# K and V gradient stores on ScalarE's DMA queue, K and V loads alone on SyncE's

## Chip, core and metric

The kernel runs on one core of one Trainium2 chip. The metric is the device time of one execution in microseconds (us). Before the change it is 723.07 us, the median of 3 runs (722.93 to 723.51).

## What is computed

The reference is one decode step of a block that adds attention over a KV cache and a gated MLP to its input, together with the gradients of everything for a given `grad_out`. One token (a row of 640) meets 32 heads with a cache of 8192 x 128 each, in bf16.

```python
q = (xn @ wq).reshape(1, 1, 32, 128)                     # xn = layernorm(x)
scores = einsum("bhqd,bhkd->bhqk", q, k) * 128 ** -0.5   # k, v: [1, 32, 8192, 128]
p = softmax(scores)
out = x + einsum("bhqk,bhkd->bhqd", p, v).reshape(1, 1, 4096) @ wo
out = out + (silu(xn @ w1) * (xn @ w3)) @ w2
outputs = out, *vjp(grad_out)     # d x, d k_cache, d v_cache, d wq, d wo, d w1, d w3, d w2
```

The gradients of K and V are as large as the caches: each head reads 2 MB of K and 2 MB of V and writes 2 MB of each gradient. With the weights and their gradients that is 151.34 MB read and 152.91 MB written.

## The kernel before

**Slots.** Ten SBUF slots of [128, 8192] bf16 (`kv0` to `kv9`, 2 MB each, L133) hold K and V tiles. A tile is loaded into a slot, used, overwritten in place by its own gradient and stored; then the slot takes another load. Four of the slots hold the MLP's weights first, until `mlp()` has run, between heads 1 and 2.

**One head** is written out by hand in `head(h)` (L834); the schedule is manual, so every engine runs its instructions in the order in which the code issues them. K is transposed in eight chunks of four 128x128 blocks by TensorE (`T`, L400 to L407) into one of three PSUM buffers `pT`, which ScalarE copies to SBUF (`KT`, L406); `Mp` (L425) multiplies the copies with the query and accumulates the scores; ScalarE takes them out (`ev`, L432). V goes the same way with the output gradient. VectorE does the softmax (row maximum `mx`, L468). The first four chunks of the next head's K are transposed already at the end of a head. The sums over the cache (`wsum`, L519) are matmuls on the untransposed tiles.

**Gradients.** `outer` (L552) overwrites a tile with an outer product on VectorE, in two halves of 2.28 us. At the start of head h VectorE does both halves of head h-1's V and the first half of its K (`outers_a`, L822); the second half of K follows after head h's softmax (`outers_b`, L828). The cast of the next query rows `qd` (`rows_act`, L462) on ScalarE comes behind that.

**Stores and loads.** `store` (L563) is called at the end of `outers_a` for V and of `outers_b` for K. It puts the gradient's store on SyncE's DMA queue (`fifo`, L106), gives the slot back to the list `free_slots` and calls `load_next` (L139), which puts the next pending K or V load on the same queue (`fifo_wide`, L111; head 0 by L106) into the slot that has been free longest. After the first loads `lag[0]` is 3: a load is only issued while at least three slots are free, so its slot's store lies two stores back. SyncE issues its DMAs in order; a load first waits until the store of its slot has landed, and whatever stands behind it waits too. From head 23 on each of 15 stores is followed by a marker: a load of 1 to 15 rows of 8 bytes of `A_x` into a small tile `marks`, which nothing reads.

**Completion.** DMAs issued by SyncE and ScalarE take turns on eight completion semaphores; a DMA that reuses one waits for the earlier DMA on it.

**Other queues.** POOL (GpSimd) issues the MLP's gradients, the weights of the later groups of four heads, and the weight gradients. The gradient of wq leaves for most groups as scatters (L372), six of `wq_g` and `rel` tiles in turn and one more for `rel`, each behind the landing of the one before; the work for one group is spread over the heads of the next (`side_k`, `side_m`, `side_v`, L770 to L803). VectorE writes `rel` at L601, and needs the scatter that read it last to have landed. ScalarE's queue carries only the two input rows at the start.

Of the kernel before, what the change touches and what calls it, by code (L numbers as in the profile page):

```python
# [9 lines left out]
BF16 = mybir.dt.bfloat16  # L10
# [11 lines left out]
def kernel(  # L22
# [22 lines left out]
    nc = tc.nc  # L45
# [14 lines left out]
    consts = ctx.enter_context(tc.tile_pool(name="consts", bufs=1))  # L60
# [16 lines left out]
    dkc = out_2.rearrange("b h (p j) d -> (b h) p (j d)", p=P)  # L77
    dvc = out_3.rearrange("b h (p j) d -> (b h) p (j d)", p=P)
# [26 lines left out]
    def fifo(out_, in_):  # L105
        nc.sync.dma_start(out_, in_)  # L106
# [21 lines left out]
        load_wq(g, eng)  # L128
        load_wo(g, eng)

    x_rows = A_x.rearrange("a b (k w) -> (a b k) w", w=40)
    marks = consts.tile([16, 15, 4], BF16, name="marks")
    free_slots = [kvpool.tile([P, KVN], BF16, name=f"kv{i}", tag=f"kv{i}") for i in range(NSLOT)]  # L133
    kv_tiles = {}
    pending = [("K", h) if k == 0 else ("V", h) for h in range(H) for k in range(2)]

    lag = [1]

    def load_next():  # L139
        if not pending or len(free_slots) < lag[0]:  # L140
            return
        kind, h = pending.pop(0)
        t = free_slots.pop(0)
        (fifo if h == 0 else fifo_wide)(t[:], (kc if kind == "K" else vc)[h])
        kv_tiles[(kind, h)] = t
# [28 lines left out]
    fifo(w3b, w3_v[:, NA, :])  # L174
    for _ in range(2):
        load_next()

    lag[0] = 3

    ident_f = consts.tile([P, P], F32, name="ident_f")  # L180
    make_identity(nc, ident_f[:])
# [49 lines left out]
    def pst():  # L231
        return ps_t.tile([P, 512], F32, name="pT", tag="pT")
# [40 lines left out]
    def prep_do(g, hh):  # L273
        G_ = grp[g]
        junk = small.tile([P, D], BF16, name="side", bufs=1)
        nc.vector.scalar_tensor_tensor(junk[:], G_["wo"][:, hh, :], 1.0, g_bc[:], ALU.mult, ALU.mult,  # L276
                                       accum_out=G_["do"][:, hh:hh + 1])
        if hh == GH - 1:
            nc.vector.tensor_copy(G_["cb"][:, 1, :], G_["do"][:])
# [117 lines left out]
    def new_head(h):  # L397
        hd[h] = dict(kt={}, qz=qz_tiles[h % 2])

    def T(h, kind, c):  # L400
        W3 = kv_tiles[(kind, h)][:].bitcast(F32).rearrange("p (i w) -> p i w", w=P)
        pT = pst()
        for k in range(4):
            nc.tensor.transpose(pT[:, k * P:(k + 1) * P], W3[:, 4 * c + k, :], ident_f[:])  # L404
        KT = kt_tile()
        nc.scalar.copy(KT[:].rearrange("p k w -> p (k w)"), pT[:])  # L406
        hd[h]["kt"][(kind, c)] = KT  # L407
# [21 lines left out]
    def ev(h, kind):  # L429
        S_ = hd[h]  # L430
        XS = kt_tile()
        nc.scalar.copy(XS[0:QH].rearrange("p k w -> p (k w)"), S_.pop(kind)[0:QH, :])  # L432
        S_["xr" + kind] = XS
# [26 lines left out]
    def rows_act(h):  # L460
        qd = small.tile([P, 2, DH], BF16, name="qd")
        nc.scalar.copy(qd[:].rearrange("p a d -> p (a d)"), hd[h].pop("ps_r"))  # L462
        hd[h]["qd"] = qd
# [63 lines left out]
    def o_sum(h):  # L527
        wsum(h, "V", 0)
# [12 lines left out]
    def col(h):  # L541
        g = h // GH
        m = hd[h]["m"]
        XS = xg.pop("XS")
        for r in range(4):
            nc.tensor.matmul(m[:, OC:OC + NS], lhsT=XS[:, r, :], rhs=mask8[:, r, :],
                             start=False, stop=(r == 3), skip_group_check=True)
        nc.scalar.copy(grp[g]["od"][:].rearrange("p h a -> p (h a)"), m[:, OC:OC + NS])

    def outer(dst, vec, pair, lo, hi):  # L550
        n = hi - lo
        nc.vector.tensor_tensor(  # L552
            dst[:, lo * DH:hi * DH].rearrange("p (j a b) -> p j a b", a=DH // 2, b=2),
            vec.rearrange("p (a b) -> p a b", b=2).unsqueeze(1).to_broadcast([P, n, DH // 2, 2]),
            pair[:, lo:hi, :].unsqueeze(2).to_broadcast([P, n, DH // 2, 2]), ALU.mult)

    def outer_v(h, lo, hi):
        outer(kv_tiles[("V", h)], hd[h]["qd"][:, 1, :], hd[h]["P2"], lo, hi)

    def outer_k(h, lo, hi):  # L560
        outer(kv_tiles[("K", h)], hd[h]["qd"][:, 0, :], hd[h]["U2"], lo, hi)

    def store(kind, h):  # L563
        t = kv_tiles.pop((kind, h))
        if kind == "K":
            hd.pop(h)
        fifo((dkc if kind == "K" else dvc)[h], t[:])
        n = 2 * (h - 23) + (kind == "K") + 1
        if 1 <= n <= 15:
            fifo(marks[0:n, n - 1, :], x_rows[0:n, 0:4])  # L570
        free_slots.append(t)
        load_next()

    dxa = consts.tile([P, NC, NG], F32, name="dxa")

    def fin_od(g):
        G_ = grp[g]
        G_["od_bf"] = small.tile([P, GH, 2], BF16, name="od_bf")
        nc.vector.tensor_scalar(G_["od_bf"][:, :, 0:1], G_["od"][:, :, 0:1], 1.0, None, ALU.mult)
        nc.vector.tensor_scalar(G_["od_bf"][:, :, 1:2], G_["od"][:, :, 1:2], scale, None, ALU.mult)  # L580
# [23 lines left out]
    def fin_wq(g, ci):  # L604
        G_ = grp[g]
        wq_g, dqb = G_["wq"], G_["dqb"]
        nc.vector.scalar_tensor_tensor(wq_g[:, ci, :], wq_g[:, ci, :], 1.0, dqb, ALU.mult, ALU.mult,  # L607
                                       accum_out=dxa[:, ci, g:g + 1])
        nc.vector.tensor_scalar(wq_g[:, ci, :], dqb, xn_col[:, ci:ci + 1], None, ALU.mult)
        if g in SCAT:  # L610
            scatter(wq_g[:, ci, :], row_idx[:, ci:ci + 1], g)
            if ci == NC - 1:
                rel_out(g, 1)
        elif g == 0:
            nc.gpsimd.dma_start(dwq_v[:, ci, 0:GW], wq_g[:, ci, :])
        elif ci == NC - 1:
            nc.gpsimd.dma_start(dwq_v[:, :, g * GW:(g + 1) * GW], wq_g[:])
        if ci == NC - 1:
            grp.pop(g)
            if g + 3 < NG:  # L620
                load_group(g + 3, nc.gpsimd)
# [148 lines left out]
    def side_k(h):  # L770
        g, hh = divmod(h, GH)
        if hh == 1 and g > 0:
            fin_wq(g - 1, 0)
        elif hh == 2 and g > 0:
            fin_wq(g - 1, 3)
        elif hh == 3 and g + 1 < NG:
            prep_do(g + 1, 1)
# [44 lines left out]
    def outers_a(h):  # L822
        outer_v(h, 0, J // 2)
        outer_v(h, J // 2, J)
        store("V", h)
        outer_k(h, 0, J // 2)

    def outers_b(h):  # L828
        outer_k(h, J // 2, J)
        store("K", h)  # L830
# [3 lines left out]
    def head(h):  # L834
        nxt = h + 1 < H
        pre = nxt and h + 1 != MLP_AT
        has_prev = h > 0 and h != MLP_AT
        had = (4 if h else 2) if h != MLP_AT else 0
        if nxt:
            new_head(h + 1)  # L840
        if has_prev:
            outers_a(h - 1)
        side_k(h)
        for c in range(had, NCH, 2):
            T(h, "K", c)
            T(h, "K", c + 1)
            if c >= 2:
                Mp(h, "K", c - 2)
            if h > 0 and h % GH == 0 and c == 4:
                col(h - 1)  # L850
        T(h, "V", 0)
        T(h, "V", 1)
        Mp(h, "K", NCH - 2)
        ev(h, "K")
        if h == 0:
            first_do()
        T(h, "V", 2)
        T(h, "V", 3)
        selm(h, "K")
        mx(h)  # L860
        Mp(h, "V", 0)
        T(h, "V", 4)
        mx_bc(h)
        side_m(h)
        T(h, "V", 5)
        Mp(h, "V", 2)
        expo(h)
        T(h, "V", 6)
        zsum(h)
        probs(h)  # L870
        if has_prev:
            outers_b(h - 1)
        side_pe1(h)
        T(h, "V", 7)
        side_pe1b(h)
        Mp(h, "V", 4)
        side_pe2(h)
        side_v(h)
        if nxt:
            fill_qz(h + 1)  # L880
            rows_pe(h + 1, pst()[:, 0:2 * DH], True)
            rows_act(h + 1)
        if pre:
            T(h + 1, "K", 0)
            T(h + 1, "K", 1)
        Mp(h, "V", NCH - 2)
        ev(h, "V")
        o_sum(h)
        selm(h, "V")
        rdot(h)  # L890
        if pre:
            T(h + 1, "K", 2)
        dsum(h)
        if pre:
            T(h + 1, "K", 3)
            Mp(h + 1, "K", 0)
        dq_sum(h)
        if not nxt:
            col(h)
# [12 lines left out]
    for h in range(H):  # L912
        if h == 6:
            rel_setup()
        if h == MLP_AT:
            outers_a(h - 1)
            outers_b(h - 1)
            mlp()
        head(h)
        if h < 2:  # L920
            nc.gpsimd.tensor_copy(gate[:], hd[h]["rdot"][:])
            load_group(h + 1, nc.gpsimd)
    outers_a(H - 1)
    outers_b(H - 1)
    fin_od(NG - 1)
    fin_pe(NG - 1)
    fin_wo(NG - 1)
# [65 lines left out]
```

## Time and profile before

| | |
|---|---|
| median of 3 runs | 723.07 us (722.93 to 723.51) |
| profiled execution | 722.83 us; span from first to last instruction 721.0 us |
| TensorE busy | 602.1 us (84%), granted clock 0.928 of full on average |
| VectorE busy | 472.2 us (65%) |
| ScalarE busy | 364.3 us (51%) |
| POOL busy | 85.1 us (12%) |
| DMA | 303.56 MB, mean 421 GB/s |
| K and V loads, stores | 64 and 64 of 2048 KB each |
| chain that ended last | DMA 45%, TensorE 39%, VectorE 10% |

The profile comes from one execution on the chip. Its page gives busy time by engine, the span in 40 slices of 18 us with the tenths in which each engine was busy and the GB/s that the DMA engines moved, the DMA queues (q1 is the queue of SyncE, q0 that of POOL), the chain of work that ended last, and the costliest groups of instructions. The trace behind it gives the same for any window: a timeline (start, duration, engine, line, operation, output <- input), the waits (who waited for whom) and busy times by stage. In a timeline PE is TensorE, DVE is VectorE, ACT is ScalarE, and SPq is SyncE's queue. A bracket at the end of a line tells how long the engine was idle before the instruction and what ended that.

### The profile page before, as it was taken

To read this page: it belongs to the slowest core of one execution; us is meant where nothing else is said; L and a number is where in the kernel's file an instruction comes from. 1 tells how busy PE (TensorE), PEld (TensorE's weight loads), DVE (VectorE), ACT (ScalarE), POOL (GpSimd) and SP (SyncE) were. 2 spreads that over 40 slices of the span, in tenths; PEclk is the share of its full clock that TensorE was granted. 3 is DMA by queue.
4 is the path that set the end of the run, shared out by engine and by line. 5 is a ranking of instruction groups with operands and counts; after the bars stand their busy time and mean duration, and the time that the engine had idled before them with its cause. 6 is when DMAs were issued, how large, how long until landed. Compare 5 with 4: busy or idle time off the path is not lost.

```text
span 721.0 us, 13243 instructions
## 1 busy us (share of the span) xinstructions
PE 602.1 (84%) x5237; PEld 376.9 (52%) x5244; DVE 472.2 (65%) x895; ACT 364.3 (51%) x726; POOL 85.1 (12%) x86
## 2 busy tenths in 40 slices
PE   6989699987999999878986899778987889978921
PEld 4556566645565556545553555445554555545510
DVE  4369927678858886767755765556774757667581
ACT  3641166653666566545554555455653556555510
POOL 0110100000101122111120111112210101111110
PEclk9987999997999999999998999899998999999965
DMA  9999999999999999999999999999999999999996
GB/s 358 400 418 413 437 428 424 425 436 428 420 425 422 431 429 428 418 434 431 423 423 430 423 430 427 423 429 430 430 419 430 427 432 427 428 432 425 424 428 295
DMA packets 23403, 303.56 MB, mean 421 GB/s; under 512 B 4054, under 2 KB 5404, under 8 KB 10156
## 3 DMA queue, kind: packets, MB, share of 16 engines
q1 hardware_dynamic: 16840, 276.39, 90.1%
q0 software_dynamic: 6496, 26.31, 9.1%
q8 instruction: 41, 0.67, 0.4%
q14 instruction: 22, 0.18, 0.1%
q10 hardware_dynamic: 4, 0.00, 0.0%
HBM read 151.34 MB, written 152.91 MB: 422 GB/s over the span
## 4 chain that ended last, share of the span: by engine, by line
DMA 45%; PE 39%; DVE 10%; ACT 3%; issue 2%; SPq 0%; ACTq 0%; DVEq 0%
DMA kv<-in_A_k_cache_dram 27%; PE pT L404 18%; DMA out_dram<-kv 13%; PE sA L425 5%; DVE kv L552 4%; PE dA L425 4%; PE X L519 4%; DMA kv<-in_A_v_cache_dram 3%; PE m L442 2%; ACT KT L406 2%; DMA out_dram<-rel,rel_idx 1%; PE gu_ps L649 1%; PE dh_ps L660 1%; PE dx_acc L747 1%; ACT KT L432 1%
## 5 line engine op out<-in xcount | busy, mean ns | idle before, releaser
L406 ACT COPY KT<-pT 128x512 f32<-128x512 f32 x512 | 288.2, 588 | 235.4 <-PE pT L404 214.8
L404 PE MATMUL pT<-ident_f,kv 128*128 128x128 f32 x2048 | 304.3, 287 | 53.9 <-DMA kv<-in_A_k_cache_dram 39.8
L404 PEld LDWEIGHTS pT<-ident_f,kv 128*128 128x128 f32 x2048 | 233.9, 147 | 144.2 <-PE pT L404 52.9
L552 DVE TENSOR_TENSOR kv<-qd,U 128x4096 bf16<-128x4096 bf16 x64 | 146.0, 2284 | 0.0
L552 DVE TENSOR_TENSOR kv<-qd,P 128x4096 bf16<-128x4096 bf16 x64 | 143.6, 2284 | 0.0
L519 PE MATMUL X<-kv,Z 128*32 128x512 bf16 x1024 | 96.8, 413 | 1.8 <-DVE Z L536 1.8
L425 PE MATMUL dA<-KT,qz 128*32 128x512 bf16 x512 | 84.9, 411 | 0.0
L425 PE MATMUL sA<-KT,qz 128*32 128x512 bf16 x512 | 82.0, 400 | 0.0
L372 POOL DMA_INDIRECT out_dram<-wq_g,row_idx x30 | 43.1, 1437 | 283.3 <-DMA out_dram<-wq_g,row_idx 108.0
L502 DVE SCALAR_TENSOR_TENSOR U<-m,P 128x64 bf16<-128x64 f32 x32 | 7.5, 235 | 94.3 <-PE m L442 94.3
L519 PEld LDWEIGHTS <-Z 128*32 128x32 bf16 x1024 | 32.7, 101 | 36.2 <-issue 9.4
L425 PEld LDWEIGHTS <-qz 128*32 128x32 bf16 x1024 | 29.5, 95 | 41.0 <-issue 38.1
L442 PEld LDWEIGHTS m<-selc,KT 64*128 64x128 f32 x256 | 21.1, 141 | 30.1 <-ACT KT L432 19.4
L442 PE MATMUL m<-selc,KT 64*128 64x64 f32 x256 | 30.0, 239 | 8.0 <-ACT KT L432 8.0
L468 DVE TENSOR_REDUCE mrow<-m 128x1 f32<-128x64 f32 x32 | 7.1, 223 | 41.7 <-PE m L442 41.4
L372 POOL DMA_INDIRECT out_dram<-rel,rel_idx x12 | 15.1, 1260 | 142.3 <-DVE rel L601 59.0
L462 ACT CAST qd<-pT 128x256 bf16<-128x256 f32 x32 | 11.9, 373 | 38.2 <-DVE kv L552 30.4
L475 DVE TENSOR_REDUCE negM<-m 128x1 f32<-128x128 f32 x32 | 9.3, 292 | 32.2 <-PE m L472 32.2
L276 DVE SCALAR_TENSOR_TENSOR side<-wo_g,g_bc 128x640 bf16<-128x640 bf16 x32 | 26.2, 819 | 2.3 <-DMA wo_g<-in_A_wo_dram 2.0
L607 DVE SCALAR_TENSOR_TENSOR wq_g<-wq_g,side 128x512 bf16<-128x512 bf16 x40 | 27.3, 683 | 0.0
L534 DVE SCALAR_TENSOR_TENSOR U<-m,P 128x128 bf16<-128x128 f32 x32 | 11.4, 355 | 15.5 <-PE m L532 15.5
L432 ACT COPY KT<-dA 64x512 f32<-64x512 f32 x32 | 18.6, 582 | 4.5 <-PE dA L425 4.5
(179 smaller groups left out, 403.9 us busy)
## 6 DMA issues: line engine op xcount, KB each, us to landing
out_dram<-kv SPq DMA_DIRECT2D x64, 2048.0 KB
kv<-in_A_k_cache_dram SPq DMA_DIRECT2D x32, 2048.0 KB
kv<-in_A_v_cache_dram SPq DMA_DIRECT2D x32, 2048.0 KB
out_dram<-wo_g POOLq DMA_DIRECT2D x8, 640.0 KB, 15.6
wq_g<-in_A_wq_dram POOLq DMA_DIRECT2D x7, 640.0 KB, 16.2
wo_g<-in_A_wo_dram POOLq DMA_DIRECT2D x7, 640.0 KB, 22.6
kv<-in_B_w_dram SPq DMA_DIRECT2D x2, 1728.0 KB
out_dram<-kv POOLq DMA_DIRECT2D x2, 1728.0 KB, 30.8
```

The source lines that it names most:

```text
L276: nc.vector.scalar_tensor_tensor(junk[:], G_["wo"][:, hh, :], 1.0, g_bc[:], ALU.mult, ALU.mult, accum_out=G_["do"][:, hh:hh + 1])
L372: nc.gpsimd.indirect_dma_start(dwq_row, bass.IndirectOffsetOnAxis(ap=idx, axis=0), src, None, element_offset=g * GW, bounds_check=(D - 1) ...
L404: nc.tensor.transpose(pT[:, k * P:(k + 1) * P], W3[:, 4 * c + k, :], ident_f[:])
L406: nc.scalar.copy(KT[:].rearrange("p k w -> p (k w)"), pT[:])
L425: nc.tensor.matmul(S_[kind][q:q + QW, :], lhsT=S_["qz"][:, o:o + QW], rhs=KTb[c][:, par, :], start=(c0 == 0 and par == 0), stop=(c0 == NCH ...
L432: nc.scalar.copy(XS[0:QH].rearrange("p k w -> p (k w)"), S_.pop(kind)[0:QH, :])
L442: nc.tensor.matmul(S_["m"][:, b0:b0 + 4 * J].rearrange("p (x c k t) -> p k x c t", x=4, k=4, t=2)[:, k], lhsT=XS[0:QH, k, :], rhs=selc[0:Q ...
L462: nc.scalar.copy(qd[:].rearrange("p a d -> p (a d)"), hd[h].pop("ps_r"))
L519: nc.tensor.matmul(xg["X"][q:q + QW, :], lhsT=Z[:, o:o + QW], rhs=W[:, N4 * i:N4 * (i + 1)], start=(slot == 0 and i < 4), stop=(slot == NS ...
L534: nc.vector.scalar_tensor_tensor(S_["U2"][:], S_["V"][:, 0:J].unsqueeze(2).to_broadcast([P, J, 2]), S_["m"][:, OC + NS:OC + NS + 1], S_["P ...
L552: nc.vector.tensor_tensor(dst[:, lo * DH:hi * DH].rearrange("p (j a b) -> p j a b", a=DH // 2, b=2), vec.rearrange("p (a b) -> p a b", b=2 ...
L607: nc.vector.scalar_tensor_tensor(wq_g[:, ci, :], wq_g[:, ci, :], 1.0, dqb, ALU.mult, ALU.mult, accum_out=dxa[:, ci, g:g + 1])
```

## The change

`store` no longer issues anything: it notes the finished tile in a list `made`. A new function `send` empties the list. For each tile it issues the store on ScalarE's DMA queue, gives the slot back and calls `load_next`. `send` is called twice in a head: behind `side_k` (so on ScalarE behind the copies of the first four chunks of K, and ahead of the others), which takes the V store, and behind `rows_act`, which takes the K store; and it is called ahead of the MLP and at the end. `load_next` issues a load as soon as one slot is free. The slot is then the one whose store was issued just before, and SyncE waits until that store has landed. SyncE's queue carries no stores of K and V any more. The markers are gone. The order on TensorE, VectorE and POOL is unchanged.

```diff
-    x_rows = A_x.rearrange("a b (k w) -> (a b k) w", w=40)
-    marks = consts.tile([16, 15, 4], BF16, name="marks")
...
-    lag = [1]
-
     def load_next():
-        if not pending or len(free_slots) < lag[0]:
+        if not pending or not free_slots:
             return
...
-    lag[0] = 3
-
...
+    made = []
+
     def store(kind, h):
-        t = kv_tiles.pop((kind, h))
+        made.append((kind, h, kv_tiles.pop((kind, h))))
         if kind == "K":
             hd.pop(h)
-        fifo((dkc if kind == "K" else dvc)[h], t[:])
-        n = 2 * (h - 23) + (kind == "K") + 1
-        if 1 <= n <= 15:
-            fifo(marks[0:n, n - 1, :], x_rows[0:n, 0:4])
-        free_slots.append(t)
-        load_next()
+
+    def send():
+        while made:
+            kind, h, t = made.pop(0)
+            nc.scalar.dma_start((dkc if kind == "K" else dvc)[h], t[:])
+            free_slots.append(t)
+            load_next()
...
         side_k(h)
+        send()
         for c in range(had, NCH, 2):
...
             rows_act(h + 1)
+        send()
         if pre:
...
             outers_b(h - 1)
+            send()
             mlp()
...
     outers_a(H - 1)
+    send()
     outers_b(H - 1)
+    send()
```

## Prediction

> **What bounds the kernel now.** I read the page's slices first (part 2: DMA share and GB/s in 40 slices).
>
> ```profile
> DMA  9999999999999999999999999999999999999996
> GB/s 358 400 418 413 437 428 424 425 436 428 420 425 422 431 429 428 418 434 431 423 423 430 423 430 427 423 429 430 430 419 430 427 432 427 428 432 425 424 428 295
> ...
> q1 hardware_dynamic: 16840, 276.39, 90.1%
> q0 software_dynamic: 6496, 26.31, 9.1%
> ```
>
> The DMA engines are full in every slice but the last. 303.56 MB at the usual 427 GB/s is 711 us of the 721.0 us span; the start (77 GB/s in the first 3 us) and the end (298 GB/s at 712 to 716 us, 60 at 716 to 721) take the rest. So the first bound is bytes, and the change moves the same bytes, the markers apart. Second, the waits, by engine and line (us in total, times, longest):
>
> ```profile
> SPq L111 <- DMA out_dram<-kv: 452.5, 56, 14.1
> ...
> PE pT L404 <- DMA kv<-in_A_k_cache_dram: 39.8, 19, 4.7
> ```
>
> SyncE stands 452 us before loads, waiting for a slot's store, and the next store waits behind it; yet TensorE lacks only 40 us of K (and 13.8 of V). Third, how much room compute has. In the chain of waits no K or V load stands between 11.7 and 301.6 us: there compute runs freely. VectorE's timeline gives the start of each head's V gradient (L552, P): 186.88, 204.70, 222.81, 240.03, 257.25, so four free heads in 70.37 us, **17.6 us a head**. From the one at 105.82 to the last at 687.30 are 29 heads in 581.5 us, 20.05 each. The head with rel_setup took 28.3, 10.7 extra. So 581.5 - 29 x 17.6 - 10.7 = 60 us is slack, **2.08 us a head**. That is the number that decides this case.
>
> **The change, part by part.**
>
> *64 stores move from SyncE to ScalarE.* ScalarE now waits for what the store waits for, and its copies out of PSUM (L406, 16 a head) queue behind it; TensorE waits for those through the three pT buffers. The order of the built kernel puts the V store behind the copies of chunks 2 and 3 of K and ahead of those of 4 and up, and the K store right behind the qd cast (L462). A free head, VectorE and then ScalarE:
>
> ```profile
> 222.81 4.49 DVE L552 TENSOR_TENSOR kv<-qd,P 128x4096 bf16<-128x4096 bf16 x2
> 227.21 2.28 DVE L552 TENSOR_TENSOR kv<-qd,U 128x4096 bf16<-128x4096 bf16 x1
> ```
>
> ```profile
> 222.24 1.21 ACT L406 COPY KT<-pT 128x512 f32<-128x512 f32 x2 [1.19 <-PE pT L404]
> 224.83 1.08 ACT L406 COPY KT<-pT 128x512 f32<-128x512 f32 x2 [1.38 <-PE pT L404]
> 226.46 1.08 ACT L406 COPY KT<-pT 128x512 f32<-128x512 f32 x2 [0.56 <-PE pT L404]
> 228.04 1.08 ACT L406 COPY KT<-pT 128x512 f32<-128x512 f32 x2 [0.50 <-PE pT L404]
> 229.04 0.58 ACT L432 COPY KT<-sA 64x512 f32<-64x512 f32 x1
> ```
>
> The V gradient ends at 227.30. Issuing a store costs ScalarE something between 0.21 us (its second row load at the start) and 0.59 (the median of SyncE's stores); I take 0.34, SyncE's stores that go out straight after a wait for VectorE. So chunk 4 is copied from 227.64 instead of 224.83: ScalarE is 2.8 us late. TensorE meanwhile fills all three buffers and needs the first one back for chunk 7: at 227.64 + 0.59 = 228.2 instead of 226.2 (the second half of the pair that began at 225.72). From there both engines go at their old pace, so the K scores (L432, 229.04) are about **2.0 us** late; VectorE's row maximum (230.41) came just behind both TensorE and its own work, and takes 1.9 of that. In one head of four the column product (L546, 1.06 us) fills part of the gap: 1.1. Together 3 x 1.9 + 1.1 = 6.8 us for four heads.
>
> *The K store* costs only its issue: the cast ahead of it already waits for the same gradient ("ACT qd L462 <- DVE kv L552", 30.4 us over 20 times). But the copies and the V evacuation behind it are on the path to the next V gradient, so 0.34 each, 1.4 for four heads. Sum 8.2 us for four heads, **2.05 us a head, against a slack of 2.08**. From below (0.21 an issue, TensorE absorbing as with the column product everywhere: 1.1) it is 1.3; from above (ScalarE's whole 2.8 plus 0.59) 3.4. I take 2.05, since each step stands on a row of a free head.
>
> What becomes of it: compute stops running ahead of the loads and no longer waits for them; it reaches its last gradient about when it did. The cover has some 8 us more at the end: the last K store goes out at 696.2, and the DMA engines have work until about 716.
>
> *Stores no longer stand behind waiting loads.* SyncE's 452 us of waits stay with SyncE, where nothing else queues now. The gain is nothing while the DMA engines are full; it counts only where they were not. At 51 to 60 us they moved 388 GB/s at shares of 0.91 to 0.96, waiting for the third free slot (first load at 67.16). With the next load sent as soon as one slot has landed that hole can close: 9 x (1 - 388/427) = 0.8 us; I take 0.4.
>
> *Rate of two queues at once.* The trace never has K loads and K stores on two queues. Nearest rows: 88 to 124 us, MLP stores on POOL's queue beside loads on SyncE's: 432 GB/s. Steady one-queue stretch 320 to 370: 428. Stores alone, 686 to 712: 425. Scatter-rich stretch 437 to 455: 421. So 421 to 432, that is +10 to -8 us over 711; I take no change, the likest row being 428.
>
> [...]
>
> *Lanes.* In the built order a store also waits for the landing of the store four before it. Two heads earlier is some 40 us; a transfer now lands 16 to 38 us after its issue (median 25.3). Nothing, unless ScalarE's queue is served much worse than SyncE's.
>
> *The 15 markers* go: 15 x 0.31 us of SyncE's time and some 60 us of its waits at L106 for K, V and the MLP's loads, next to waits for the slots anyway (575.19 a marker, 580.13 the next load, which waited for its slot). Nothing; at most the last engine's lag at 716 to 721 changes by a us or two either way.
>
> Sum: -0.4, plus 29 x (2.05 - 2.08) = -0.9 that the DMA bound does not pay out, plus about 1 us for two bounds that now touch each other: 722.83 (the profiled execution, span 721.0 and 1.8 around it) + 0.6 = **723.4 us**. The median of the runs is 723.07, 0.2 above that execution. 0.2%, about 1.4 us, is what can be told from no change.
>
> **Rivals.**
>
> *Faster: two queues pack better.* 432 instead of 427 GB/s: 703 instead of 711 us, so about 715. For: the 88 to 124 row. Against: 73 to 127, the same mix, gave 428. It also needs compute to come earlier by as much, and compute has just lost its slack. Chance 0.2.
>
> *Slower: ScalarE's wait costs more than the slack.* Place: the V store ahead of chunk 4. It decides from 2.08 + 8/29 = 2.35 us a head. At 2.7 it is 29 x 0.62 - 8 = 10 us: 733; at the upper end, 3.4, 30 us: 753. For: my 2.05 has no margin, and TensorE's gap at chunk 7 grows from none to 2 us. Against: part of a head's late work can be absorbed as in the head with the column product. Chance 0.27.
>
> *Slower: POOL's scatters.* They form a chain, each waiting for the landing of the one before:
>
> ```profile
> 388.53 1.02 POOL L372 DMA_INDIRECT out_dram<-wq_g,row_idx  x1 [17.38 <-DVE rZ L492]
> ...
> 434.88 0.98 POOL L372 DMA_INDIRECT out_dram<-rel,rel_idx  x1 [8.36 <-issue]
> ...
> 455.35 1.20 POOL L372 DMA_INDIRECT out_dram<-rel,rel_idx  x1 [17.80 <-DVE rel L601]
> ```
>
> Six of them land by 434.88 + 9.4 = 444.3, and VectorE next writes rel (L601) at 455: 11 us to spare, 1.8 us for each scatter of 9.3. If a third busy queue makes each 2.5 us longer, VectorE stops 6 x 2.5 - 11 = 4 us in each of five groups: 20 us, near 742. For: 7.0 to 19.2 us from issue to landing already. Against: the bytes in flight are bounded by the same ten slots. Chance 0.12.
>
> [...]
>
> *It does not do what it says* (lanes hold ScalarE and the order stays): 723. Chance 0.01.
>
> **How the numbers follow.** The forecast, bound by bytes, has 0.40, with its own range 719 to 727; by my shares 0.13 of it fall below 721.6, 0.13 within 0.2%, 0.14 above. With 0.2 for two queues on the one side and 0.39 for the two stalls on the other: faster 0.33, same 0.14, slower 0.53. The range 713 to 743 takes in the faster case to 433 GB/s, the scatters, and ScalarE's cost to 3.05 us a head (29 x 0.97 - 8 = 20); what it leaves out is 0.03 below and 0.13 above.
>
> **What would show it.** Right: ScalarE idle some 2 to 3 us before L406 with VectorE's L552 as releaser, in every head; heads of 19 to 20 us from the start; few waits of TensorE for K; GB/s still 425 to 430 to the end. ScalarE's cost too low: GB/s falling below 420 after some 600 us, no waits for K at all, the last gradient after 695. Scatters: waits of VectorE L601 for rel. Two queues: 431 or more in every slice. Wrong altogether would be long waits of ScalarE for stores landing, which I hold for nothing here.

## The result and the profile after

The changed kernel takes **763.29 us** (median of 4 runs, 759.21 to 763.75), beside 723.21 us for the kernel before on the same chip: a ratio of 1.054 (95% interval 1.0505 to 1.0578), 40 us slower. The prediction was 723.4 with a range of 713 to 743; it was wrong. The profiled execution has a span of 761.5 us, 40.5 more than before. Of one kernel below, `v_late_lag3`, two of four executions fell into a slower state and are left out of its ratio.

The lines of the slices and queues of the changed kernel, from its page (q10 is ScalarE's queue; a slice is now 19 us):

```profile
DMA  9999999999999999999999999999999999965557
GB/s 365 399 422 422 431 426 428 405 432 404 403 399 438 422 423 428 422 430 423 442 417 422 426 432 429 425 427 403 407 422 395 433 429 423 416 288 240 236 222 289
...
q1 hardware_dynamic: 7384, 142.17, 44.7%
q10 hardware_dynamic: 9220, 134.22, 41.6%
q0 software_dynamic: 6496, 26.31, 8.7%
```

The stores are indeed on a queue of their own. While both queues are busy the rate is nearly what it was: 422 GB/s on average from 38 to 665 us, beside 427 from 36 to 712 us before. The loss is seen in the last five slices: from 665 us on the DMA engines are busy to 0.62 and move 256 GB/s. The last K or V load goes out at 661.34 us; the slots then hold tiles that compute has still to work off, and only its stores are left to move. The end is set by compute, which is what bounds this kernel now. TensorE hardly waits for K any more (once, 0.9 us, where it was 39.8).

The waits of the changed kernel, by engine and line (us in total, times, longest), beside SyncE's:

```profile
ACT KT L400 <- DVE kv L546: 120.7, 28, 15.0
...
PE pT L398 <- ACT KT L400: 48.6, 29, 4.0
...
DVE rel L598 <- DMA out_dram<-rel,rel_idx: 32.5, 3, 14.2
```

```profile
SPq L111 <- DMA out_dram<-kv: 579.0, 56, 18.6
```

(Lines from L400 on stand six lower than before for `T` and `Mp`, three lower for `rel`: L398 and L400 are the old L404 and L406, L546 is `outer`, L598 is `rel`, L366 the scatter, L567 the store in `send`.) The first two are the wait that the change puts on ScalarE, and TensorE's wait behind it, nearly once in each head. The third had hardly been there: VectorE waits for a scatter three times, where in the kernel before it did so once, for 2.60 us.

One head without other waits, ScalarE's timeline from its first gap on:

```profile
269.94 0.34 ACTq L567 DMA_DIRECT2D out_dram<-kv  x1
270.32 2.05 ACT L400 COPY KT<-pT 128x512 f32<-128x512 f32 x4 [4.26 <-DVE kv L546]
272.85 1.07 ACT L400 COPY KT<-pT 128x512 f32<-128x512 f32 x2 [0.48 <-PE pT L398]
```

ScalarE has stood 4.26 us for the V gradient; then the store goes out (0.34 us, the duration that the prediction took), and four copies that had waited follow in one block.

**Where the 40.5 us come from.** VectorE's timeline gives the start of each V gradient. From 109.17 to 738.03 us, 29 heads take 628.9 us, where before they took 581.5. Heads that wait for nothing else take 19.7 us (17.6 forecast as free head, plus 2.05). Sorted by length: 29 x 19.7 = 571.3; the head with rel_setup 12.1 more; nine heads of 21.2 to 22.2 us, 16.5 more together; three heads of 24.1, 31.8 and 33.0 us, 29.8 more; the rest -0.8. Up to the first of them the start is 3.3 us later, and what follows the last one is 10.2 us shorter (33.7 before, 23.5 after): 3.3 + 47.4 - 10.2 = 40.5.

The nine heads of 21.2 to 22.2 us show a slower TensorE. Its timeline at two chunks of K, in a head of 19.7 us and in the next, of 21.6:

```profile
270.95 0.66 PE L398 MATMUL pT<-ident_f,kv 128*128 128x128 f32 x4 [1.98 <-ACT KT L400]
272.10 1.09 PE L398 MATMUL pT<-ident_f,kv 128*128 128x128 f32 x8
...
290.61 0.87 PE L398 MATMUL pT<-ident_f,kv 128*128 128x128 f32 x4 [1.99 <-ACT KT L400]
292.38 1.97 PE L398 MATMUL pT<-ident_f,kv 128*128 128x128 f32 x8
```

The gap is the same 2 us. Behind the second the same eight transposes take 1.97 us instead of 1.09, and the granted clock of that head is 0.92 instead of 1.00 (windows 285.10 to 306.70 and 265.42 to 285.10); from 290.9 to 294.3 us it is 0.50. The two longest heads, of 33.0 and 31.8 us, each have a wait of VectorE for `rel` in them, 14.2 and 13.1 us. For the second, VectorE's timeline, then POOL's in the group of heads before it, shows where it is from:

```profile
677.24 0.35 DVE L598 TENSOR_SCALAR rel<-side,rel_x 128x512 bf16<-128x512 bf16 x1 [13.06 <-DMA out_dram<-rel,rel_idx]
```

```profile
573.94 0.90 POOL L119 DMA_DIRECT2D wq_g<-in_A_wq_dram  x1
574.84 0.81 POOL L124 DMA_DIRECT2D wo_g<-in_A_wo_dram  x1
583.35 1.14 POOL L366 DMA_INDIRECT out_dram<-rel,rel_idx  x1 [7.70 <-DVE wo_g L594]
584.49 0.78 POOL L595 DMA_DIRECT2D out_dram<-wo_g  x1
614.42 1.03 POOL L366 DMA_INDIRECT out_dram<-wq_g,row_idx  x1 [29.16 <-DMA out_dram<-rel,rel_idx]
```

The scatter issued at 583.35 lands after 30 us, and the six others of its chain follow only then, up to the one for which VectorE waits until 677. It stands 8 us behind two weight loads of POOL's own queue. These loads now take 21.8 (`wq_g`) and 33.0 us (`wo_g`) from issue to landing, by the list of DMA issues; before it was 16.2 and 22.6. The median scatter has hardly changed: 9.2 us for `wq_g` and 10.1 for `rel`, 8.9 and 9.1 before. The right comparison for the one at 583.35 is not this median: in the kernel before, the two `rel` scatters that went out 7 us behind such loads (292.85 and 369.18) landed after 19.2 and 18.6 us. So the same place costs about 11 us more, as much as the landing of `wo_g` has grown. The scatter at 410.54 took 29.6 us in it; the one at 504.65, just when VectorE had stood for 14 us, 17.9.

### The profile page after: what moved, and what is told of

Read it like the earlier page. It is cut to its first block, busy times and chain, and to the rows that moved or that the text cites. A ratio compares the mean times of both kernels' runs of the same rounds, so it can differ in the third digit from the quotient of the medians.

```text
span 761.5 us, 13315 instructions
## 1 busy us (share of the span) xinstructions
PE 612.5 (80%) x5244; PEld 380.4 (50%) x5244; DVE 472.3 (62%) x895; ACT 361.3 (47%) x726; POOL 78.4 (10%) x86
## 2 busy tenths in 40 slices
DMA packets 23162, 303.55 MB, mean 399 GB/s; under 512 B 3814, under 2 KB 5164, under 8 KB 9916
## 3 DMA queue, kind: packets, MB, share of 16 engines
q1 hardware_dynamic: 7384, 142.17, 44.7%
## 5 line engine op out<-in xcount | busy, mean ns | idle before, releaser
L400 ACT COPY KT<-pT 128x512 f32<-128x512 f32 x512 | 285.8, 590 | 294.1 <-PE pT L398 155.4
L398 PE MATMUL pT<-ident_f,kv 128*128 128x128 f32 x2048 | 316.3, 292 | 49.4 <-ACT KT L400 48.6
L398 PEld LDWEIGHTS pT<-ident_f,kv 128*128 128x128 f32 x2048 | 238.4, 150 | 148.9 <-PE pT L398 59.5
L546 DVE TENSOR_TENSOR kv<-qd,U 128x4096 bf16<-128x4096 bf16 x64 | 146.0, 2284 | 0.0
L546 DVE TENSOR_TENSOR kv<-qd,P 128x4096 bf16<-128x4096 bf16 x64 | 143.6, 2285 | 0.0
L513 PE MATMUL X<-kv,Z 128*32 128x512 bf16 x1024 | 93.6, 403 | 1.8 <-DVE Z L530 1.8
L419 PE MATMUL sA<-KT,qz 128*32 128x512 bf16 x512 | 88.0, 426 | 0.0
L419 PE MATMUL dA<-KT,qz 128*32 128x512 bf16 x512 | 81.0, 395 | 0.0
L366 POOL DMA_INDIRECT out_dram<-wq_g,row_idx x30 | 38.0, 1268 | 321.9 <-DMA out_dram<-wq_g,row_idx 125.2
L419 PEld LDWEIGHTS <-qz 128*32 128x32 bf16 x1024 | 29.6, 95 | 42.1 <-issue 39.2
L436 PEld LDWEIGHTS m<-selc,KT 64*128 64x128 f32 x256 | 20.6, 138 | 49.0 <-ACT KT L426 43.7
L526 PE MATMUL m<-rdot,masks 128*128 128x1 f32 x64 | 10.5, 233 | 29.1 <-DVE U L496 29.1
L366 POOL DMA_INDIRECT out_dram<-rel,rel_idx x12 | 13.6, 1130 | 124.3 <-DVE wo_g L594 61.9
L526 PEld LDWEIGHTS m<-rdot,masks 128*128 128x128 f32 x64 | 10.1, 198 | 30.2 <-DVE U L496 30.1
## 6 DMA issues: line engine op xcount, KB each, us to landing
out_dram<-wo_g POOLq DMA_DIRECT2D x8, 640.0 KB, 20.6
wq_g<-in_A_wq_dram POOLq DMA_DIRECT2D x7, 640.0 KB, 21.8
```

The lines of the kernel that those rows point to most:

```text
L366: nc.gpsimd.indirect_dma_start(dwq_row, bass.IndirectOffsetOnAxis(ap=idx, axis=0), src, None, element_offset=g * GW, bounds_check=(D - 1) ...
L419: nc.tensor.matmul(S_[kind][q:q + QW, :], lhsT=S_["qz"][:, o:o + QW], rhs=KTb[c][:, par, :], start=(c0 == 0 and par == 0), stop=(c0 == NCH ...
L436: nc.tensor.matmul(S_["m"][:, b0:b0 + 4 * J].rearrange("p (x c k t) -> p k x c t", x=4, k=4, t=2)[:, k], lhsT=XS[0:QH, k, :], rhs=selc[0:Q ...
L513: nc.tensor.matmul(xg["X"][q:q + QW, :], lhsT=Z[:, o:o + QW], rhs=W[:, N4 * i:N4 * (i + 1)], start=(slot == 0 and i < 4), stop=(slot == NS ...
L526: nc.tensor.matmul(S_["m"][:, OC + NS:OC + NS + 1], lhsT=negones_b, rhs=S_["rdot"][:], start=False, stop=True, skip_group_check=True)
L546: nc.vector.tensor_tensor(dst[:, lo * DH:hi * DH].rearrange("p (j a b) -> p j a b", a=DH // 2, b=2), vec.rearrange("p (a b) -> p a b", b=2 ...
```

## The experiments

Two theories came out of this. **S**: ScalarE's wait ahead of the V store costs the time, with the slower clock that follows TensorE's gap. **P**: two big queues leave POOL's queue a smaller share; its weight loads take longer, and the chain of seven scatters a group, one of which stands behind them, becomes the bound through VectorE's wait for `rel`. Times are medians with their lowest and highest run, ratios to runs of the kernel before on the same chip (723.2 to 723.4 us), with 95% intervals. The expectations also name a theory **Q**, that two queues at once, or loads sent early, are slow by themselves; in experiment 6 the letter stands for the loads ahead of the scatter.

### 1. The V store late: `v_late`

```diff
         side_k(h)
-        send()
...
         ev(h, "K")
+        send()
```

> The changed kernel with the first send of a head moved behind the copy of the K scores out of PSUM, so that ScalarE no longer stands before the V gradient is done. Theory S (ScalarE's stand before the V store, with TensorE's gap and its slower clock behind it, is most of the loss): the free head falls from 19.66 to about 17.9 us, no head with a clock of 0.92 on that account, and the time to 721 to 732, with waits of VectorE for rel still there. Theory P (POOL's scatters are the loss, ScalarE's wait lies beside other work): heads shorter but rel waits of over 30 us stay or grow, 738 to 750. Theory Q (two queues at once, or loads sent early, are slow by themselves): 750 or more, whatever ScalarE does.

754.64 us (752.38 to 756.19), ratio 1.0419 (1.0399 to 1.0440). Most heads are back at 17.4 to 18.4 us, and still only 8.7 us are regained. The time lies 4.6 us above the range of P and in that of Q; the waits for `rel` are those that P named. They and POOL's timeline show where the gain went:

```profile
DVE rel L598 <- DMA out_dram<-rel,rel_idx: 81.1, 5, 27.2
```

```profile
402.77 1.15 POOL L366 DMA_INDIRECT out_dram<-rel,rel_idx  x1 [7.12 <-DVE wo_g L594]
403.92 0.77 POOL L595 DMA_DIRECT2D out_dram<-wo_g  x1
436.43 1.02 POOL L366 DMA_INDIRECT out_dram<-wq_g,row_idx  x1 [31.74 <-DVE P L488]
...
493.58 0.98 POOL L366 DMA_INDIRECT out_dram<-rel,rel_idx  x1 [7.38 <-issue]
494.55 0.90 POOL L119 DMA_DIRECT2D wq_g<-in_A_wq_dram  x1
495.45 0.80 POOL L124 DMA_DIRECT2D wo_g<-in_A_wo_dram  x1
503.29 1.15 POOL L366 DMA_INDIRECT out_dram<-rel,rel_idx  x1 [7.05 <-DVE wo_g L594]
```

Here the chain sets the pace. From the `rel` scatter behind one group's loads to that behind the next are 100.5 us (402.77 to 503.29), and four heads, three of 18 to 20 us and one of 44.7, take just as long (19.6 + 18.1 + 18.2 + 44.7 = 100.6). VectorE waits for the last scatter, writes `rel` at once, and the next scatter goes out right behind the loads. It doesn't go on so in every group: the scatter at 503.29 stands as close behind its loads, and the next one goes out 10.4 us after it instead of 33.7, just when VectorE had stood for 27.2 us and the DMA engines moved only 390 GB/s (slice of 509 to 528 us). That group takes 73 us, and VectorE doesn't wait for the chain at its end; at the end of the next one it waits 26.1 us again. In the kernel before, VectorE's and POOL's timelines show the reserve between the same instructions, none in one group and some in a later one:

```profile
292.16 0.35 DVE L601 TENSOR_SCALAR rel<-side,rel_x 128x512 bf16<-128x512 bf16 x1 [2.60 <-DMA out_dram<-rel,rel_idx]
```

```profile
521.64 0.90 POOL L119 DMA_DIRECT2D wq_g<-in_A_wq_dram  x1
522.77 0.81 POOL L124 DMA_DIRECT2D wo_g<-in_A_wo_dram  x1 [0.23 <-PE X L519]
539.53 1.21 POOL L372 DMA_INDIRECT out_dram<-rel,rel_idx  x1 [15.95 <-DVE rel L601]
```

In the later group the `rel` scatter waits for VectorE and not the other way round; it goes out 17 us behind the loads, which land after 16.9 and 22.5 us. So faster compute only waits longer: S alone cannot explain the result.

### 2. Another buffer for the last scatter: `rel_apart` and `v_late_rel_apart`

The write that waits was to go into a tile that is free by then.

```diff
     def rel_out(g, s):
-        nc.vector.tensor_scalar(rel[:], grp[g]["dqb"], rel_x[:, s:s + 1], None, ALU.mult)
-        scatter(rel[:], rel_idx[:, s:s + 1], g)
+        to = grp[g]["wq"][:, 0, :] if s else rel[:]
+        nc.vector.tensor_scalar(to, grp[g]["dqb"], rel_x[:, s:s + 1], None, ALU.mult)
+        scatter(to, rel_idx[:, s:s + 1], g)
```

> The changed kernel with the second rel block of a group written into the part of wq_g whose scatter landed first, so that VectorE never waits for the scatter of that block before it writes the next rel. Theory S and P together (their costs add): the 32.5 us of waits go, and as compute ends last, the time falls by about as much, to 728 to 738. S alone (the waits only take the place of others): 750 to 763. Q: 750 or more.

> Both edits. S and P together: compute runs at about 17.9 us a head with no rel waits, so bytes bound the kernel again: 714 to 722. Q: 740 or more, as both kernels' edits leave the two queues and the early loads as they are.

Alone on the changed kernel: 780.88 us (775.02 to 785.67), ratio 1.0781 (1.0714 to 1.0848). With the late V store: 770.82 (767.36 to 771.27), ratio 1.0640 (1.0611 to 1.0669). Both are slower, because the edit missed its aim: the tile is not free. Its own scatters have not landed, and the wait only moved. The waits of the second:

```profile
DVE wq_g L599 <- DMA out_dram<-wq_g,row_idx: 89.2, 4, 29.4
```

This tells nothing against P or for it, except that where VectorE waits for the chain, the time follows.

### 3. ScalarE's wait alone, on one queue: `wait_alone` and `wait_warm`

The kernel before, with a copy of one column of the finished V gradient at the place of `send`: ScalarE waits as in the changed kernel, and all DMAs stay where they were. The second (the last four lines) also adds matmuls of zeros to a sum where TensorE would stand idle.

```diff
         side_k(h)
+        if has_prev:
+            nc.scalar.copy(tick[:], last_v.pop()[:, KVN - 1:KVN])
...
+            if c == 6 and has_prev:
+                for _ in range(14):
+                    nc.tensor.matmul(acc[0:28, 0:DHALF], lhsT=Z[:, 0:28], rhs=g_bc[:, 0:DHALF], start=False, stop=True,
+                                     skip_group_check=True)
```

> The kernel before, with its one queue, and with a copy of one column of the V gradient on ScalarE where the changed kernel sends the V store: the wait for VectorE alone, no DMA moved. S: heads of 19.3 to 21.5 us from the start, TensorE's gap of about 2 us at chunk 7, and 728 to 745, the slack of 2.08 us a head being used up by the wait, the copy and the slower clock. P and Q: within 5 us of before, since queue and scatters are untouched.

> wait_alone (one queue, ScalarE's wait alone) with 14 matmuls of zeros into acc on TensorE between chunks 6 and 7 of K, where it stands still for 2 us in that kernel: nothing is changed in what acc holds, but TensorE does not idle there. If the slower clock behind that gap is the difference between heads of 19.1 and of 20.6 to 21.4 us, all heads take 19.1 to 19.6 and the time falls from 730.8 to 722 to 726, bound by bytes. If those heads are long for another reason: 729 to 734.

`wait_alone`: 730.78 us (727.04 to 731.91), ratio 1.0083 (1.0054 to 1.0112). Its waits:

```profile
ACT tick L849 <- DVE kv L552: 117.5, 30, 14.6
...
PE pT L404 <- ACT KT L406: 46.4, 30, 3.4
```

They are those of the changed kernel (120.7 and 48.6 us) to within 5%, and they cost 7.4 us. Heads take 19.1 us, or 20.6 to 21.4, which is so in 18 of the 29. `wait_warm`: 725.13 us (724.52 to 726.72), ratio 1.0028 (1.0018 to 1.0038); its granted clock is 0.962 instead of 0.92, and its heads from 239 to 654 us take 19.4 to 20.3 us, but for two, though ScalarE's wait is unchanged at 117.6 us. So 5.5 of the 7.4 us go with the slower clock, and 2 us are left for the wait itself, which on one queue the slack nearly covers, as the prediction had it. S is real, and small.

### 4. No scatters: `v_late_plain`, `after_plain`, `before_plain`

The gradient of wq leaves by plain transfers, as it does for the first and last group anyway. Nothing is left out by this: the same gradient is written (where the texts on record speak of work left out, they are wrong), only `rel` and the scatters go.

```diff
-    SCAT = range(1, NG - 1)
+    SCAT = range(0)
```

> The late V send, and the gradient of wq stored by plain DMAs for every group (SCAT empty) instead of by scatters and rel blocks: the same values leave, with no chain of landings and no rel to wait for. Theory P as it stands now (POOL's queue gets a smaller share beside two big queues, its weight loads land after 33 us instead of 22.6, the scatter behind them after 30, and VectorE waits for rel, up to 27 us at a time): 712 to 726, bound by bytes again, heads of 17.5 to 18.5 us until loads run short. Theory Q (two queues or early loads are slow by themselves): 740 or more.

> The changed kernel, ScalarE's early wait left in, with plain stores of the gradient of wq as above. P and S: only ScalarE's part is left, which cost 7.4 us on the old queue (wait_alone, without the 0.34 us that the K send takes in each head), so 730 to 742, with heads of 19.6 and 21.2 to 21.6 us. S as the larger part: 745 to 760. Q: 750 or more.

> The kernel before, with the gradients of wq and wk stored by plain transfers instead of the scatters (so these gradients miss what the scatters add; work is left out). Control for the two kernels of two queues without scatters. Theory P (two big queues make POOL's scatter chain the bound): on one big queue that chain had 11 us to spare in each group, so without it nothing is gained beyond its own bytes: 719 to 723.5 us, and then the step from here to the changed kernel without scatters (737.95) is the price of ScalarE's wait alone, 14 to 19 us. Rival (scatters slow any version by the traffic of their small packets): 698 to 712, about as much below 723.2 as the two versions of two queues fell (23 to 25 us).

| scatters | one queue | two queues, V store late | two queues, as changed |
|---|---|---|---|
| as they were | 723.2 | 754.64 (1.0419) | 763.29 (1.0542) |
| none | 731.25 (1.0113: 1.0096 to 1.0129) | 731.83 (1.0128: 1.0111 to 1.0145) | 737.95 (1.0223: 1.0194 to 1.0253) |

This table settles most of it. Without scatters a second queue costs nothing that can be told (731.83 beside 731.25), and ScalarE's wait 6.1 us more, close to the 7.4 of experiment 3 and inside what P and S gave `after_plain`. With scatters the second queue costs 31.4 us. So 31 of the 40 us need both the second queue and the scatters (31.4 less 0.6), as P has it. The control missed both of its expectations: on one queue plain transfers are 8 us slower than scatters. TensorE waits 27.0 us for V there, 13.8 in the kernel before; why was not followed up.

The time of `v_late_plain` is 6 us above what P gave it, which the 8 us of the control would cover. It also shows the wait that the prediction had called "wrong altogether". ScalarE's waits:

```profile
ACT KT L400 <- DMA out_dram<-kv: 37.4, 13, 4.7
```

A store lands 41 to 45 us after its issue here (pieces of the chain of waits), long enough to hold up the store four later on the same completion semaphore: eight such pieces follow one another from 280.58 to 626.2 us, while 16 heads send 32 stores. The changed kernel itself has no such wait.

### 5. Packet size and loads in flight: `v_late_narrow`, `v_late_lag3`

With 64 rows a tile, loads go in packets of 32 KB, the stores in packets of 16: from 583 to 585 us of the changed kernel, 16 packets of 0.52 MB together on SyncE's queue and 16 of 0.26 MB on ScalarE's. What the expectation calls turns by packet is seen in the kernel before: while POOL's weight loads and the scatter behind them are under way, SyncE's queue and POOL's move nearly the same number of packets, 183 and 179 from 293 to 303 us, 178 and 177 from 370 to 380. With three queues in the changed kernel it is less even: 97 on SyncE's, 96 on ScalarE's and 73 on POOL's from 401 to 411 us, and 84, 107 and 121 from 421 to 431. The first edit makes the loads' rows 16 KB too; the second brings back the old rule of three free slots for a load.

```diff
-    kc = A_k_cache.rearrange("b h (r n) d -> (b h) r (n d)", r=RD)
+    kc = A_k_cache.rearrange("b h (r n) d -> (b h) r (n d)", r=P)
...
-        (fifo if h == 0 else fifo_wide)(t[:], (kc if kind == "K" else vc)[h])
+        fifo(t[:], (kc if kind == "K" else vc)[h])
```

```diff
-        if not pending or not free_slots:
+        if not pending or len(free_slots) < lag[0]:
...
+    lag[0] = 3
```

> The late V send with K and V loads read as 128 rows of 16 KB instead of 64 rows of 32 KB, so that packets of the load queue are as big as those of the store queue. P with turns by packet: a POOL packet waits for 16 + 16 KB instead of 32 + 16, so the weight loads land after about 27 us instead of 33, waits for rel fall from 81 to 20 to 55 us, and the time from 754.6 to 730 to 748. P without turns by packet (share by bytes or by order): 750 to 758. Q: 750 to 758.

> The changed kernel with both stores late (ScalarE does not wait for VectorE; 754.64 us), and each load sent only when three slots are free, as before the change: still two big queues, but fewer loads in flight. If early loads crowd POOL's queue (rival E): waits of VectorE for rel fall from 81 us to under 30, wo_g loads land after 25 us or less instead of 32, time 726 to 738. If it is the second busy queue whatever is in flight (theory P): waits for rel stay at 60 us or more, wo_g loads at 29 us or more, time 748 to 760.

`v_late_narrow`: 746.22 us (742.51 to 751.91), ratio 1.0317 (1.0254 to 1.0380), 8 us less than `v_late`. The time is inside what turns by packet gave; the rows behind it moved less than expected: VectorE's waits for `rel` 73.4 us (81.1), `wo_g` loads 31.8 us (33.7). The direction is the expected one: smaller packets of the loads, a shorter chain. But halving them (11352 packets on SyncE's queue instead of 7384) takes back only 2 us of the 11 that `wo_g` loads lost, so turns by packet alone don't give the size.

`v_late_lag3`: ratio 1.0297 (1.0248 to 1.0345), 745 us on average (741.67 and 747.64). Its waits, from a longer execution of 757 us, so that only their kind is read:

```profile
DVE rel L602 <- DMA out_dram<-rel,rel_idx: 86.4, 5, 30.4
```

Its `wo_g` loads land after 32.8 us there. With fewer loads in flight the wait for the chain is still the longest that VectorE has, which speaks for the second busy queue. But the time lies 3 us under P's range and 7 above the rival's, 10 us less than `v_late`: that early loads have no part in it is not shown.

### 6. The weight loads out of POOL's queue: `v_late_load_sp`, `after_load_sp`, `before_load_sp`

Open until here was the step: is the one scatter behind the weight loads the cause, or is every scatter slower?

```diff
             if g + 3 < NG:
-                load_group(g + 3, nc.gpsimd)
+                load_group(g + 3, nc.sync)
```

> The changed kernel with late V stores (754.64 us), and the weights of the later groups (wq_g and wo_g, 640 KB each, five groups) loaded on SyncE's queue instead of POOL's; all scatters stay. Theory Q (the scatter of rel waits behind these loads in POOL's own queue, and the chain of seven closes on itself): no scatter lands after more than 20 us, VectorE's waits for rel fall from 81 us to under 20, time 724 to 735. Rival (each scatter is slower beside two big queues, wherever the loads are): waits for rel of 50 us or more, time 745 to 757.

> The changed kernel (763.29 us) with the weights of the later groups loaded on SyncE's queue instead of POOL's. Theory Q: waits for rel go from 32.5 us to under 10 and ScalarE's wait with the slower clock is left, 6 to 8 us a run more than late V stores with the same loads: 729 to 742 us. Rival: waits for rel near 30 us, time 753 to 765.

> The kernel before with the weights of the later groups loaded on SyncE's queue instead of POOL's; control. The chain has its reserve there and DMA engines are full, so nothing is to be gained: 721 to 725 us. If these loads hold back K and V loads behind them (each waits for its tile's last scatter or store, some 10 to 16 us, five times): 726 to 735 us.

`v_late_load_sp`: 735.03 us (731.74 to 736.88), ratio 1.0152 (1.0120 to 1.0185), 20 us less than `v_late`, with all scatters in place, at the upper edge of what the theory gave it. Its waits:

```profile
ACT KT L400 <- DMA kv<-in_A_v_cache_dram: 51.8, 5, 11.5
...
DVE rel L598 <- DMA out_dram<-rel,rel_idx: 17.2, 5, 4.7
```

Five waits for `rel` are left, of at most 4.7 us instead of 27. The median scatter takes 10.6 and 8.8 us, no less than in `v_late` (9.7 and 9.2). So scatters are not slower in general: the one behind the weight loads was. What the move brings in itself is the first line: K and V loads now stand behind five pairs of weight loads, each of which waits for its tile, and ScalarE stands for V loads that it never issued (by the shared semaphores, below). On one queue the move costs about as much, there by TensorE's waits for V (33.6 us instead of 13.8): the control `before_load_sp` takes 732.45 us (731.07 to 733.71), ratio 1.0126 (1.0109 to 1.0143), the second of its two cases. Beside it two queues with late V stores cost 2.6 us (735.03 less 732.45).

`after_load_sp`: 763.87 us (762.10 to 765.32), ratio 1.0553 (1.0536 to 1.0571). Here each expectation fails by half. The waits for `rel` are gone from its list, as the theory has it, and the time is what it was, as the rival has it. In their place ScalarE waits for weight loads that it never issued:

```profile
ACT KT L400 <- DMA wq_g<-in_A_wq_dram: 29.3, 4, 8.6
```

SyncE's and ScalarE's DMAs share eight completion semaphores (in the trace of the kernel before, each of the 150 after the first eight has that of the eighth ahead of it), so a store on ScalarE can wait for a weight load on SyncE; four heads take 24.1 to 27.2 us. The experiment exchanged one stall for another and doesn't separate the theories on this kernel; `after_plain` does.

### 7. Markers, and a filler in the changed kernel: `no_marks`, `keep_warm`

```diff
-        if 1 <= n <= 15:
-            fifo(marks[0:n, n - 1, :], x_rows[0:n, 0:4])
```

`keep_warm` puts the matmuls of zeros of experiment 3 into the changed kernel.

> The kernel before without its 15 marker loads, nothing else changed. By my step on the markers: 722 to 724.5 us. Rival (they hold back loads near the end so that the stores keep their share, and the changed kernel loses part of its end by their absence): 726 to 735 us, and stores alone on the DMA engines at the end at under 300 GB/s.

> The changed kernel with 14 matmuls of zeros added to a sum between chunks 6 and 7 of K, where TensorE stands waiting for ScalarE (they add zero). If the two losses trade off (scatter chain P and compute S: faster compute waits longer for rel): free heads 19.3 to 20.3 us and a granted clock of 0.95 or more, but waits for rel 45 us or more instead of 32.5, time 756 to 764. If the losses simply add: the same heads, waits for rel near 32, time 752 to 756.

`no_marks`: 723.20 us (722.48 to 724.82), ratio 1.0003 (0.9993 to 1.0012). The markers are worth nothing, as forecast.

`keep_warm`: 768.52 us (765.33 to 773.83), ratio 1.0647 (1.0594 to 1.0701). This is inconclusive. TensorE's waits for ScalarE's copies fall from 48.6 us to 1.7, but the mean granted clock rises only from 0.92 to 0.936, heads without such a wait still take up to 21.9 us, and VectorE's waits for `rel` stay at 31.7. Its time is above both expectations, and why it is slower than the changed kernel was not found. That the clock accounts for the nine longer heads of the changed kernel is therefore shown by its trace and, on one queue, by experiment 3, not by removing it there.

No version here beats the kernel before by more than can be told.

## Why the prediction was wrong, point by point

- **What bounds the kernel now: right for the kernel before.** The forecast rested on compute having room; the room it found (2.08 us a head and about 8 us at the end) was really there: `wait_alone` uses it up and loses 2 us beside the clock's 5.5. What it left out is the room of POOL's chain, below.
- **The V and K store on ScalarE: right in mechanism and size, as far as it went.** 2.05 us a head was forecast; free heads take 19.66 to 19.7 us instead of 17.22 to 17.6, 2.1 to 2.4 more. The 0.34 us an issue holds to the digit; ScalarE's wait stands where the text put it, in 28 heads; it is idle for 4.26 us there, 2.9 more than the 1.38 of the row before, beside the 2.8 of the text.
- **A missing term: TensorE's clock.** The text let both engines go on "at their old pace" after a gap of 2.0 us. The gap came out at that (1.98 to 1.99 us in the heads shown), but in nine heads (gaps of 1.98 to 2.06 us, in one of them 4.04) the clock fell to 0.50 for 3.4 us, in that one for 6.8: 16.5 us together in the changed kernel's list of heads. On one queue, where part of it is hidden, the time shows 5.5 us of it.
- **"It reaches its last gradient about when it did": the step that failed.** The last V gradient starts at 738.03 us, not near 687.30. The sum has no term for POOL's chain, on the ground that it has 11 us to spare in each of five groups. That was read from one group, at 455. The two groups ahead of it had next to nothing to spare: at 292.16, at the end of the stretch where compute runs freely, VectorE waited 2.60 us for the scatter, and at 368.55 it wrote `rel` 9.6 us after the scatter of 358.99 went out, which took 9.2. In place of a term of nothing the runs show 31 us, which need both the second queue and the scatters (experiment 4), of which 20 go when the weight loads leave POOL's queue (experiment 6).
- **The rival of POOL's scatters was the right one, at 0.12 and with the wrong price.** It named the wait (VectorE at `rel`) and the place. It spread the cost evenly, 2.5 us on each of six scatters, and the argument against it was that the bytes in flight are bounded by the ten slots. The runs show the median scatter longer by 0.3 to 1.0 us only, and one of the seven, in two of the five groups, at 30 us instead of 19, since it stands behind two weight loads, the later of which went from 22.6 to 33.0 us. What it had to ask was what is ahead of a scatter in its own queue. It also overlooked that a late chain feeds itself: when VectorE has to wait for `rel`, it writes it as soon as it may, and the next scatter stands right behind the loads. By which of these steps the price of 20 us became 31 is not shown one by one. From 742 the rival comes to 754.64 with the V store late, and 763.29 with ScalarE's wait on top.
- **Rate of two queues at once: nearly right.** 422 GB/s on average up to 665 us, and 424 to 428 in the stretches of `v_late_plain` from 90 to 640 us, beside 427 before: inside the 421 to 432 of the text, at its lower end. The faster rival did not happen, and compute had no room for it.
- **Stores no longer behind waiting loads, -0.4: not separately seen.** In the third and fourth slice, about where the hole lay, the rate is 422 instead of 418 and 413 GB/s, which fits it; no run tried it alone.
- **Lanes: nothing in the changed kernel, as forecast,** but 37.4 us of waits in `v_late_plain`, so the margin was thin.
- **Markers: right,** 0.0 us beside an interval of 0.1%.
- **What would show it:** the sign of the scatter rival came true, waits of VectorE for `rel`. So did all signs of the other slower rival, ScalarE's cost too low: hardly a wait for K, GB/s low after 660 us, the last gradient after 695. Those three appear whenever compute comes late and did not separate the two; `v_late` and the table of experiment 4 did.

Open: why two busy queues stretch a 640 KB weight load by as much as 10 us while the total rate is nearly unchanged (loads in packets of half the size took back 2 us of it), and why `keep_warm` gains nothing.

## What to carry to other kernels

Moving bulk transfers to a second queue moved no more bytes here (303.55 MB, 303.56 before, at 422 GB/s beside 427), but it shifted shares (`wo_g` loads landed after 33.0 us instead of 22.6): look at every other queue that is busy at the time, find the chain of small dependent transfers in it, and ask for each of them what stands ahead of it in its own queue. A transfer issued from a compute engine takes that engine's place in line: what it waits for, everything behind it on that engine waits for too (here ScalarE's copies, 120.7 us in 28 waits). When an engine gets faster or slower, check whether a chain that had a reserve of a few us still has it, and in every stretch, not in one; once the reserve is gone, the gain of the faster engine is only waited away (`v_late`: 81.1 us of waits for `rel` instead of 32.5).

## What the hardware showed that was not expected

- With a gap of about 2 us in TensorE's work its clock was sometimes halved: eight transposes take 1.97 us behind it instead of 1.09, and the granted clock is 0.50 for 3.4 us (290.9 to 294.3). It was so in the nine longer heads of the changed kernel (gaps of 1.98 to 2.06 us, in one head 4.04), while eight others with a gap of 1.98 to 1.99 us kept 1.00; what decides is not shown. In `wait_alone` 18 of 29 heads are longer by as much, at a mean clock of 0.92; with matmuls of zeros in the gap (`wait_warm`) it is 0.962.
- With loads in packets of 32 KB and stores in packets of 16 on two queues, loads ran ahead of compute (the last one left at 661.34 us with 100 us of span to go), and the end was left to stores at 222 to 240 GB/s.
- Small transfers on a third queue were hardly slowed by a second big queue (0.3 to 1.0 us at the median), 640 KB loads on it by 6 to 10 us, and a small one that stood 7 to 9 us behind such loads by 11 (19 to 30 us, in two cases of three).
